# u's block built by ScalarE, fewer clearings, and another order of issue in an attention and two-MLP kernel

## The chip, the cores and the metric

The kernel runs on one core of a Trainium2 chip. The metric is the device time of one execution in microseconds (us). The profiler records one execution; its span runs from the first to the last instruction and is a little shorter than the execution's own time. The engines are named as in the profile: PE is TensorE's matmuls and PEld its weight loads, DVE is VectorE, ACT is ScalarE, POOL is GpSimd, SP is SyncE, on whose queue nearly all loads and stores are issued.

## The reference

All is fp32. A linear attention with a decay per channel runs over 768 steps, for 2 batches and 8 heads of 48 channels; its output, as 1536 tokens of 384 channels, goes through an MLP with ELU (2048 wide) and then through four experts (1024 wide, ReLU), whose outputs are weighted by normalized probabilities.

```python
    for t in range(S):
        kt, vt, rt, wt = (k[:, :, t], v[:, :, t], r[:, :, t], w[:, :, t])
        cur = np.einsum('bhd,bhe->bhde', u[None] * kt, vt)
        y[:, :, t] = np.einsum('bhd,bhde->bhe', rt, state + cur)
        state = wt[:, :, :, None] * state + np.einsum('bhd,bhe->bhde', kt, vt)
...
    h = x @ w_in
    g = np.where(h > 0.0, h, alpha * (np.exp(np.minimum(h, 0.0)) - 1.0))
    return (g @ w_out).astype(np.float32)
...
    p = domain_probs / (domain_probs.sum(-1, keepdims=True) + 1e-09)
    for e in range(E):
        h = np.maximum(x @ w1[e], 0.0)
        out += p[:, e:e + 1] * (h @ w2[e])
```

## The kernel before

**Attention.** The 768 steps are cut into chunks of 128: six for each batch, twelve in all, numbered 0 to 11 so that even ones belong to batch 0 and odd ones to batch 1 (`SEQ`). The eight heads lie in four pairs along the partitions (`heads`). A chunk `i` goes through small steps, each a function of `attn(i)` with a two-letter name that the order uses: `iw`, `ik`, `lv` load decays, keys with r, and v; `su` and `pr` are VectorE scans for the decays to the chunk's end and from its start; `kd` and `rd` multiply keys and r by them; `g` multiplies r by the keys in place; `tr` transposes kd on TensorE, with a ScalarE copy; `pa` are the scores; `ow` multiplies g by u's block, which sums it over a head's channels; `am` masks the scores, with VectorE (D), with a ScalarE copy and a GpSimd select (S), or one of each (M); `vo` multiplies ow's result by v; `pp` and `us` update the state, `ws` decays it; `py` multiplies masked scores by v and r by the state; `ys` adds vo's; `xs` splits the result into a rounded part (a ScalarE copy) and a rest (a subtraction); `xd` spreads rows of it by two DMAs.

**ELU block.** Tokens lie in three blocks of four chunks (`BLOCKS`). Step `n` of 48 stands for a quarter of the hidden width `q = n // 12`, the token block `n // 4 % 3`, and a tile `f = n % 4`. `h` is the first product (nine matmuls of 128x512, three passes of split operands for each of three parts of 128 channels) with ScalarE's ReLU and exponential, `e` the ELU on VectorE with a ScalarE copy of its rounded part, `el` the subtraction for its rest, `z` the second product (nine matmuls into three banks). `dr`, behind a quarter's fourth `z`, adds the banks to `x2`; in the last quarter it also splits the sum again into `x`, which the experts read: dr39 for block 0, dr43 for block 1, dr47 for block 2. The weights come as 32 pieces: `wl` loads one, `wa`, `wb` and `wc` take its words apart and split them.

**Experts.** For each expert and each token block eight first products (L468) alternate with second products (L442), one tile late; `hl` is a tile with the ReLU's rounded part (ScalarE, L471) and its rest (VectorE, L472). `load_w` splits the experts' weights with ScalarE copies and VectorE subtractions; four weight buffers (`wpool`) serve both blocks in turn, so an expert's weights can only be split once a buffer of the ELU block is free. The experts' code is not part of the order written by hand.

**What sets the order.** `ORDER` is a list of 565 steps, each a name, a number and, where there is a choice, the engine (A ScalarE, D VectorE, P GpSimd). `do` issues them in this order; every engine takes its own instructions in the order in which they were issued, and semaphores enforce the data dependences. The order before ends with `z47 dr47A dr39D`. The tile `a` of `pr` has one buffer, `kr` and `w` of the loads have two; PSUM has eight banks.

Ahead of the list stand the constants (L77 to L102): VectorE fills the scans' start values, GpSimd builds the masks, u2 (a column of u for each head of a pair) from u_sb, and `ublock` from u2 by broadcast copies. L168 to L171 clear four state tiles of 128x208, of which the last 16 columns are only ever read as padding.

Of the kernel before, what the change touches and what calls it, by code (L numbers as in the profile page):

```python
# [40 lines left out]
ik6 ys2 rd3D iw5 ow4 xs2P su6 us1 ow3 vo4 xs1P pa3 ik5 xd1 iw7 pr6 vo3 am3S kd6P rd6P py4 ws3A lv6 tr6A su5 tr3A wl2  # L41
wb0P g6P pp4 lv5 wb1D us4 py3 kd5P iw8 pp3 pr5 ys4 us3 ow6 tr5A pp6 ys3 pp5 rd5P pa5 ws6A wl17 xs3P wc1D ik7 wa2D xd3
g5P am5S wc0P wa3D su7 vo6 ik8 pr7 su8 pa6 xd2 iw9 am6M xs4P ow5 rd7P ws5A vo5 wb2D py5 kd7D wc2P wb3D py6 us5 us6 ws7A
kd8P tr7A g7P wc3P pa7 h2 wl19 wl18 ys6 ws8A h1 ys5 xd4 g8P lv7 xs5P ik9 ow7 su9 tr8A am7D wa17D wa18D pr8 e1 wb17D
rd8P pr9 el1P xs6P ow8 h0 vo7 wc17P lv8 e0 el0P py7 h3 pp8 pa8 kd9D pp7 iw10 xd5 rd9P us7 us8 tr9A ys7 z0 pa9 g9P xd6
iw11 z1 xs7P am8M lv9 e2 vo8 ik10 ws9D wa19D am9M su10 wb18P wb19P xd7 kd10P el2P ow9 vo9 pp9 g10P ik11 us9 py8 py9 wl4
# [18 lines left out]
def kernel_body(ctx, tc, wkr, vv, uu, w_in, w_out, w1, w2, dp, out):  # L65
# [125 lines left out]
    def attn(i):  # L191
# [62 lines left out]

        def own_scores():

            b["po"] = bank()
            for p in range(NPAIR):
                if i in SUMMED:
                    nc.tensor.matmul(b["po"][:, 2 * p:2 * p + 2], lhsT=b["k"][:, p], rhs=u2[:, p], start=True, stop=True)  # L260
                else:
                    nc.tensor.matmul(heads(b["po"])[:, p], lhsT=ublock[:, p], rhs=b["k"][:, p], start=True, stop=True)  # L262
# [11 lines left out]

        def own_values():

            if i in SUMMED:
                vo = tile_of("vo", 1, (P, 8, D))
                nc.vector.tensor_tensor(vo, b["vs"][:, 0:8 * D].rearrange("q (h d) -> q h d", h=8),
                                        b["po"][:, 0:8].unsqueeze(2).to_broadcast([P, 8, D]), ALU.mult)  # L280
            else:
                mul("D", tile_of("bv", 2), heads(b["po"]), b["v"])
# [18 lines left out]
        def values():  # L301
            b["py"] = py = heads_bank()

            both = [(p, j) for p in range(NPAIR) for j in range(2)]
# [4 lines left out]
            for p, j in both:
                h = 2 * p + j  # L310
                nc.tensor.matmul(py[64 * j:64 * j + 64, p, :], lhsT=b["vs"][:, D * h:D * h + 64],  # L311
                                 rhs=b[f"am{j}"][:, p, :], start=first and p == 0, stop=i not in SUMMED, skip_group_check=True)
            if i in SUMMED:
                for p, j in both:
                    nc.tensor.matmul(py[64 * j:64 * j + D, p, :], lhsT=b["vo"][:, 2 * p + j], rhs=ident,
                                     start=False, stop=True, skip_group_check=True)
# [288 lines left out]
```

## Time and profile before

| | us |
|---|---|
| median of 3 executions (706.32 to 708.93) | 706.48 |
| the profiled execution's own time | 706.21 |
| its span | 704.4 |
| PE busy | 669.3 |
| DVE busy | 338.5 |
| ACT busy | 235.8 |
| POOL busy | 194.3 |

A row of the page or of a table gives busy time and a count of instructions. In a timeline a row is a run of like instructions on one engine: its start, how long it lasted, engine, line, operation, output and input, and in brackets how long the engine had been idle ahead of it and what released it. PEclk is the clock that TensorE was granted, as a share of 2.4 GHz; the low level is half of that.

### The profile page before, as it was taken

The page shows a single profiled execution, that of the slowest core. Times are in us where ns is not written, and L with a number is a line of the kernel's source. Part 1 is how long each engine was busy: PE and PEld are TensorE (multiplying, and loading weights), DVE is VectorE, ACT ScalarE, POOL GpSimd, SP SyncE. Part 2 cuts the span into 40 slices and gives each one's busy share as a digit, 9 for nine tenths or more (in the row PEclk, how much of TensorE's full clock was granted, in tenths as well). Part 3 has the DMA queues.
Part 4 walks back from the last instruction along what each step waited for, and adds up shares of the span by engine and source line. Part 5 has one row for each costly group of instructions (what it writes and reads, how often), then busy time and mean ns, then how long its engine had stood idle before and what let it go on. Part 6 is the DMA issues. An engine that isn't in the chain of part 4 may idle for free.

```text
span 704.4 us, 8788 instructions
## 1 busy us (share of the span) xinstructions
PE 669.3 (95%) x3440; PEld 550.3 (78%) x3440; DVE 338.5 (48%) x518; ACT 235.8 (33%) x454; POOL 194.3 (28%) x166
## 2 busy tenths in 40 slices
PE   6877999999999999799999999999999999999994
PEld 4766878878888788678888888888888888888883
DVE  6876987756557763631223522123872134421212
ACT  1343554766556655511113311113311123211110
POOL 7696884124444343420000002020202020210200
PEclk8779999999999999989999999999999999999997
DMA  6645462552211220110001210002350001000101
GB/s 240 202 148 197 140 204 80 171 225 80 77 50 51 80 67 1 45 46 1 0 1 45 92 44 0 1 0 91 93 177 1 0 30 62 0 15 31 45 2 49
DMA packets 19383, 50.81 MB, mean 72 GB/s; under 512 B 2504, under 2 KB 3704, under 8 KB 19204
## 3 DMA queue, kind: packets, MB, share of 16 engines
q1 hardware_dynamic: 19188, 50.15, 22.4%
q8 instruction: 29, 0.48, 0.3%
q14 instruction: 22, 0.18, 0.1%
q10 hardware_dynamic: 144, 0.00, 0.0%
HBM read 46.58 MB, written 2.38 MB: 70 GB/s over the span
## 4 chain that ended last, share of the span: by engine, by line
PE 85%; POOL 5%; DVE 4%; DMA 2%; ACT 1%; issue 1%; POOLq 0%; DVEq 0%; ACTq 0%
PE bank L468 28%; PE bank L442 28%; PE bank L363 13%; PE bank L343 11%; POOL x L113 2%; PE bank L262 1%; PE bank L311 1%; PE bank L252 1%; PE bank L307 1%; DMA v<-in_vv 1%; POOL hl L113 1%; PE bank L245 1%; POOL am L272 1%; DMA raw<-in_w_out 1%; POOL kr L110 0%
## 5 line engine op out<-in xcount | busy, mean ns | idle before, releaser
L472 DVE SCALAR_TENSOR_TENSOR hl<-bank,hl 128x512 fp32r<-128x512 f32 x96 | 66.3, 690 | 257.9 <-ACT hl L471 254.1
L471 ACT ACTIVATE hl<-bank 128x512 fp32r<-128x512 f32 x96 | 57.4, 598 | 305.2 <-PE bank L468 305.2
L454 POOL TENSOR_TENSOR x<-o,x 128x512 f32<-128x512 f32 x24 | 31.1, 1320 | 333.0 <-DVE o L452 333.0
L343 PE MATMUL bank<-x,w 128*128 128x512 f32 x432 | 103.9, 391 | 1.3 <-DVE e L351 1.3
L363 PE MATMUL bank<-hl,w 128*128 128x512 f32 x432 | 104.2, 391 | 0.7 <-DVE e L351 0.3
L343 PEld LDWEIGHTS bank<-x,w 128*128 128x128 f32 x432 | 80.6, 188 | 18.8 <-ACT w L117 1.7
L363 PEld LDWEIGHTS bank<-hl,w 128*128 128x128 f32 x432 | 80.6, 188 | 18.7 <-ACT kdt L117 0.8
L468 PE MATMUL bank<-x,w_e0a 128*128 128x512 f32 x216 | 55.0, 400 | 5.0 <-POOL x L113 2.9
L351 DVE SCALAR_TENSOR_TENSOR e<-e,bank 128x512 f32<-128x512 f32 x48 | 32.4, 683 | 49.0 <-ACT e L347 48.9
L113 POOL TENSOR_TENSOR hl<-e,hl 128x512 fp32r<-128x512 f32 x28 | 39.9, 1428 | 49.8 <-ACT hl L117 43.4
L468 PEld LDWEIGHTS bank<-x,w_e0a 128*128 128x128 f32 x216 | 41.7, 194 | 14.7 <-POOL x L113 3.3
L468 PE MATMUL bank<-x,w_e2a 128*128 128x512 f32 x216 | 53.0, 390 | 0.0
L442 PE MATMUL bank<-hl,w_e0b 128*128 128x512 f32 x216 | 53.0, 389 | 0.0
L468 PE MATMUL bank<-x,w_e1a 128*128 128x512 f32 x216 | 52.9, 389 | 0.0
L442 PE MATMUL bank<-hl,w_e1b 128*128 128x512 f32 x216 | 52.9, 389 | 0.0
L442 PE MATMUL bank<-hl,w_e2b 128*128 128x512 f32 x216 | 52.9, 389 | 0.0
L468 PE MATMUL bank<-x,w_e3a 128*128 128x512 f32 x216 | 52.8, 389 | 0.0
L442 PE MATMUL bank<-hl,w_e3b 128*128 128x512 f32 x216 | 52.7, 389 | 0.0
L442 PEld LDWEIGHTS bank<-hl,w_e0b 128*128 128x128 f32 x216 | 40.5, 188 | 8.6 <-DVE hl L472 0.2
L468 PEld LDWEIGHTS bank<-x,w_e1a 128*128 128x128 f32 x216 | 40.5, 188 | 8.4
L442 PEld LDWEIGHTS bank<-hl,w_e3b 128*128 128x128 f32 x216 | 40.5, 188 | 8.4
L442 PEld LDWEIGHTS bank<-hl,w_e2b 128*128 128x128 f32 x216 | 40.5, 188 | 8.4
(101 smaller groups left out, 838.2 us busy)
## 6 DMA issues: line engine op xcount, KB each, us to landing
kr<-in_wkr SPq DMA_DIRECT2D x12, 512.0 KB, 3.9
raw<-in_w_in SPq DMA_DIRECT2D x16, 384.0 KB, 3.2
raw<-in_w_out SPq DMA_DIRECT2D x16, 384.0 KB, 3.4
v<-in_vv SPq DMA_DIRECT2D x12, 456.0 KB, 3.8
w<-in_wkr SPq DMA_DIRECT2D x12, 258.5 KB, 3.6
gw<-in_wkr SPq DMA_DIRECT2D x12, 258.0 KB, 2.7
pr<-rows SPq DMA_DIRECT2D x1, 3072.0 KB
out<-x SPq DMA_DIRECT2D x9, 256.0 KB, 2.0
```

The costliest lines, as they stand in the source:

```text
L113: engines[e].tensor_tensor(o, a, b.bitcast(F32), ALU.subtract)
L245: nc.tensor.transpose(pt[:, p, :], b["kd"][:, p, :], ident)
L252: nc.tensor.matmul(pa[j][:, p, :], lhsT=b["kd"][64 * j:64 * j + D, p, :], rhs=b["rd"][64 * j:64 * j + D, p, :], start=True, stop=True)
L262: nc.tensor.matmul(heads(b["po"])[:, p], lhsT=ublock[:, p], rhs=b["k"][:, p], start=True, stop=True)
L343: nc.tensor.matmul(ph, lhsT=wi[:, sa, f, kk, :], rhs=x[:, kk, c0:c0 + nch, sm], start=(kk == 0 and i == 0), stop=(kk == 2 and i == 2))
L351: nc.vector.scalar_tensor_tensor(b["e"], b["e"], -1.0, b["ph"], ALU.add, ALU.max)
L363: nc.tensor.matmul(pxs[q, bl][d], lhsT=wo[:, sa, f, d * P:(d + 1) * P], rhs=b["t"][:, sm], start=(f == 0 and i == 0), stop=(f == 3 and i = ...
L442: nc.tensor.matmul(sums[d], lhsT=w[:, sa, f % 4, d * P:(d + 1) * P], rhs=t[:, sm], start=(f == 0 and i == 0), stop=(f == 7 and i == 2))
L454: (nc.vector if last else nc.gpsimd).tensor_tensor(x2[:, d, s], o, x2[:, d, s], ALU.add)
L468: nc.tensor.matmul(ph, lhsT=wt_[:, sa, kk, (f % 4) * P:(f % 4 + 1) * P], rhs=x[:, kk, 4 * b:4 * b + 4, sm], start=(kk == 0 and i == 0), st ...
L471: nc.scalar.activation(out=t[:, 0, :], in_=ph, func=AF.Relu)
L472: nc.vector.scalar_tensor_tensor(t[:, 1, :], ph, 0.0, t[:, 0, :].bitcast(F32), ALU.max, ALU.subtract)
```

## The change

The constant `half` has ones in its two diagonal quarters of 64x64, and four ScalarE activations multiply it by u's columns to give `ublock`; u2 and its GpSimd copies go. One tile `sball` takes the place of the four state tiles, and one memset clears the last 16 columns of each; the rest of a state tile is written before it is read. A variant that no chunk used (`SUMMED` was empty) is deleted. The order is written anew: the same 565 steps, some on other engines, with the last quarter's dr39 between z39 and z47 instead of at the end.

```diff
 ORDER = """
-iw0 ik0 su0 kd0P pr0 rd0P g0P iw1 su1 pr1 pa0 lv2 ik1 wl0 lv0 wl16 ow0 rd1D kd1P am0M vo0 iw2 wa16D iw4 g1P ik2 wb16P
-ik4 su2 pa1 kd2P g2P tr0A wl1 lv1 iw3 pr2 tr1A py0 ow1 tr2A pp0 rd2P su4 ow2 am1M ys0 kd4P us0 pp2 xs0P ws2A ik3 pr4
-us2 pa2 vo1 pp1 am2M vo2 su3 rd4P g4D wa0D iw6 py1 wa1D wc16P kd3D py2 g3P pa4 xd0 wl3 am4S tr4A pr3 lv4 ys1 lv3 ws4A
...
-e43 e37 z36 h38 h44 e38 el43P z43 h39 el37D z37 el38P dr43D e39 el39P z38 e44 h47 el44P h46 z39 z44 e47 el47D z45 e46
-el46D z46 z47 dr47A dr39D
+iw0 su0 ik0 iw1 ik1 wl0 kd0P iw2 pr0 rd0P g0P su1 wl1 ow0 pr1 rd1P tr0A su2 pr2 wa0D wl16 wa16D lv0 ik2 lv2 kd1P iw4
+g1D pa0 rd2P pp0 am0D vo0 kd2P tr1A pa1 wb0P iw3 su4 ow1 g2P wl2 ik4 pr4 tr2A pa2 py0 am2S ow2 lv1 ys0 kd4P ik3 us0
+ws2A vo2 g4P wb16D su3 am1D pr3 rd4P iw5 xs0P pp2 py2 lv4 us2 pp1 ow4 ys2 kd3P ik5 tr4A rd3P wc0P vo1 py1 g3P ys1 us1
...
+e40 dr35D wc14P wb15D h37 z31 wa31D el40P e37 e41 wb31P wc15P el37P dr31D z40 h42 h38 e38 wc30D el41P e42 h43 z36 e43
+z37 h44 wc31P el42P el43P el38D z41 h39 e44 e39 z42 h46 z38 z43 el44D dr43D el39D h45 z44 e45 z39 el45P dr39A e46 h47
+z45 el46D z46 e47 el47D z47 dr47A
 """.split()
...
-    u2 = const.tile([P, NPAIR, 2], F32, name="u2")
-    nc.gpsimd.memset(u2, 0.0)
+    half = const.tile([P, P], F32, name="half")
+    nc.gpsimd.memset(half, 0.0)
     for j in range(2):
-        nc.gpsimd.tensor_copy(u2[64 * j:64 * j + 64, :, j:j + 1], u_sb[64 * j:64 * j + 64])
+        nc.gpsimd.memset(half[64 * j:64 * j + 64, 64 * j:64 * j + 64], 1.0)
     ublock = const.tile([P, NPAIR, P], F32, name="ublock")
     for p in range(NPAIR):
-        nc.gpsimd.tensor_copy(ublock[:, p].rearrange("q (j c) -> q j c", j=2), u2[:, p].unsqueeze(2).to_broadcast([P, 2, 64]))
+        nc.scalar.activation(out=ublock[:, p], in_=half, func=AF.Copy, scale=u_sb[:, p])
...
-    sb = [[apool.tile([P, 208], F32, name=f"sb{b}{i}") for i in range(2)] for b in range(2)]
-    for b in range(2):
-        for i in range(2):
-            nc.gpsimd.memset(sb[b][i], 0.0)
+    sball = apool.tile([P, 4, 208], F32, name="sball")
+    nc.gpsimd.memset(sball[:, :, NPAIR * D:], 0.0)
+    sb = [[sball[:, 2 * b + m] for m in range(2)] for b in range(2)]
```

## Rows read from the trace of the kernel before

**Rows 1.** The page: busy time, share of the span, instructions of TensorE.

```profile
PE 669.3 (95%) x3440; PEld 550.3 (78%) x3440; DVE 338.5 (48%) x518; ACT 235.8 (33%) x454; POOL 194.3 (28%) x166
```

**Rows 2.** Stages: length, busy us (instructions) by engine, granted clock, DMA share, GB/s.

```profile
0.00:90.00 90.00, 71.54 (x673) 57.75 (x673) 71.72 (x96) 34.62 (x80) 72.01 (x70) 0.85 0.58 189
90.00:288.00 198.00, 196.39 (x1009) 161.85 (x1010) 125.42 (x200) 117.63 (x220) 82.56 (x67) 1.00 0.30 93
288.00:306.31 18.31, 13.27 (x49) 10.01 (x47) 11.72 (x15) 6.22 (x12) 8.70 (x6) 0.81 0.29 86
306.31:693.03 386.72, 386.72 (x1708) 319.91 (x1707) 125.73 (x203) 77.34 (x143) 31.05 (x24) 1.00 0.11 33
```

**Rows 3.** Timeline from 284 to 307 us, where the experts begin.

```profile
284.38 10.36 PE L363 MATMUL bank<-hl,w 128*128 128x512 f32 x45
...
293.42 3.85 DVE L372 TENSOR_TENSOR x<-bank,x 128x512 f32<-128x512 f32 x6 [3.11 <-PE bank L363]
...
294.86 8.70 POOL L113 TENSOR_TENSOR x<-x,x 128x512 fp32r<-128x512 f32 x6 [10.23 <-ACT x L117]
...
296.92 0.73 PE L468 MATMUL bank<-x,w_e0a 128*128 128x512 f32 x2 [2.17 <-ACT x L117]
297.18 5.24 DVE L113 TENSOR_TENSOR w_e0b<-raw_e0b,w_e0b 128x384 fp32r<-128x384 f32 x4
...
300.51 5.80 PE L468 MATMUL bank<-x,w_e0a 128*128 128x512 f32 x16 [2.86 <-POOL x L113]
```

**Rows 4.** Timeline of the first 14 us: SyncE, VectorE, GpSimd and ScalarE.

```profile
1.26 0.42 SPq L210 DMA_DIRECT2D kr<-in_wkr  x1
...
3.86 1.23 DVE L223 TENSOR_TENSOR_SCAN z<-w,first 128x516 f32<-128x516 f32 x1 [1.29 <-DMA w<-in_wkr]
...
4.07 1.25 POOL L99 COPY u<-u_sb 64x4 f32<-64x4 f32 x2 [2.05 <-DMA u_sb<-in_uu]
...
5.69 2.62 POOL L102 COPY ublock<-u 128x128 f32<-128x128 f32 x4
6.49 1.25 DVE L223 TENSOR_TENSOR_SCAN z<-w,first 128x516 f32<-128x516 f32 x1
...
8.26 0.47 POOL L171 MEMSET sb<- 128x208 f32 x2
8.70 1.17 POOL L110 TENSOR_TENSOR kd<-kr,z 128x512 f32<-128x512 f32 x1
...
11.04 2.28 DVE L230 TENSOR_TENSOR_SCAN a<-w,start 128x516 f32<-128x516 f32 x1 [3.08 <-POOL rd L110]
...
12.20 2.11 POOL L110 TENSOR_TENSOR kd<-kr,z 128x512 f32<-128x512 f32 x1
...
13.21 0.60 ACT L117 ACTIVATE am<-bank 128x512 f32<-128x512 f32 x1 [10.69 <-PE bank L252]
```

**Rows 5.** Timeline at 245 us: a short wait of TensorE inside the ELU block.

```profile
245.52 2.30 PE L343 MATMUL bank<-x,w 128*128 128x512 f32 x9 [1.26 <-DVE e L351]
```

**Rows 6.** Groups up to 300 us: busy us, mean ns | idle before; DMA: size, landing.

```profile
L125 ACT ACTIVATE sb<-sb,z 128x48 f32<-128x48 f32 x36 | 9.0, 327 | 0.0
...
L110 DVE TENSOR_TENSOR am<-bank,mask 128x512 f32<-128x512 f32 x12 | 7.9, 676 | 2.0 <-PE bank L252 2.0
...
kr<-in_wkr SPq DMA_DIRECT2D x12, 512.0 KB, 3.9
```

**Rows 7.** Waits of TensorE and SyncE: us in total, times, longest us.

```profile
PE bank L245 <- POOL kd L110: 4.7, 1, 4.7
...
PE bank L292 <- DMA v<-in_vv: 3.4, 2, 2.4
...
SPq L210 <- PE bank L262: 17.7, 7, 6.6
```

**Rows 8.** Timeline at 29 us: the decayed r of chunk 4 on GpSimd.

```profile
29.28 1.18 POOL L110 TENSOR_TENSOR rd<-kr,a 128x512 f32<-128x512 f32 x1
```

**Rows 9.** Timeline at 71 us: the first two first products of the ELU block.

```profile
71.50 4.39 PE L343 MATMUL bank<-x,w 128*128 128x512 f32 x18
```

More of the change, by code (lines that the diff above doesn't have):

```diff
@@ L32 @@
 WARM = 3
-SUMMED = set()
 ORDER = """
-iw0 ik0 su0 kd0P pr0 rd0P g0P iw1 su1 pr1 pa0 lv2 ik1 wl0 lv0 wl16 ow0 rd1D kd1P am0M vo0 iw2 wa16D iw4 g1P ik2 wb16P
-ik4 su2 pa1 kd2P g2P tr0A wl1 lv1 iw3 pr2 tr1A py0 ow1 tr2A pp0 rd2P su4 ow2 am1M ys0 kd4P us0 pp2 xs0P ws2A ik3 pr4
-us2 pa2 vo1 pp1 am2M vo2 su3 rd4P g4D wa0D iw6 py1 wa1D wc16P kd3D py2 g3P pa4 xd0 wl3 am4S tr4A pr3 lv4 ys1 lv3 ws4A
-ik6 ys2 rd3D iw5 ow4 xs2P su6 us1 ow3 vo4 xs1P pa3 ik5 xd1 iw7 pr6 vo3 am3S kd6P rd6P py4 ws3A lv6 tr6A su5 tr3A wl2
@@ L42 @@
[L42 to L46, printed above, removed]
@@ new lines @@
+g1D pa0 rd2P pp0 am0D vo0 kd2P tr1A pa1 wb0P iw3 su4 ow1 g2P wl2 ik4 pr4 tr2A pa2 py0 am2S ow2 lv1 ys0 kd4P ik3 us0
+ws2A vo2 g4P wb16D su3 am1D pr3 rd4P iw5 xs0P pp2 py2 lv4 us2 pp1 ow4 ys2 kd3P ik5 tr4A rd3P wc0P vo1 py1 g3P ys1 us1
+xd0 pa4 xs2P ws4A iw6 am4D su5 wl3 pa3 xs1P ik6 tr3A lv3 vo4 am3S xd1 xd2 su6 iw7 pp4 lv5 kd5P ow3 pr6 ws3A wa1D wa3D
+vo3 us4 wb1P py4 rd6P kd6D wb3P pp3 lv6 ik7 g5P ws6A py3 pr5 ys4 ys3 wc1D us3 g6P su7 xs3P pa6 xd3 wc16D rd5P tr5A tr6A
+am6M ow6 vo6 ws5A xs4P wa2D ow5 pp5 iw8 pa5 kd7D py6 ik8 lv7 ys6 pp6 g7P am5S tr7A ow7 us5 us6 pr7 vo5 wl18 su8 lv8
@@ new lines @@
+rd7P kd8D wb2P wc2P xs6P py5 ys5 h0 ws8A pr8 wl19 iw9 ik9 wl17 pa7 ws7A wc3D wa18D xd4 h1 wl4 wa19D am7D vo7 e1 wb18P
+rd8P tr8A pp7 lv9 g8P us7 e0 h3 el1P su9 xd6 py7 wa17D xs5P h2 el0D pa8 ow8 kd9D z0 ik10 wb17P am8D e2 iw10 wc17P g9D
+vo8 pp8 iw11 py8 pr9 ws9A us8 e3 tr9A ys7 ys8 el2D rd9P xs7D su11 wb19P wc19D xd5 z1 el3D xd7 wc18P pa9 ik11 ow9 wl6
+vo9 am9S xs8P su10 pp9 lv11 kd10P pr10 z2 g10P us9 kd11P rd10D g11P wl20 py9 z3 dr3A h4 pr11 e4 lv10 wl5 h5 ys9 pa10
+ws11A h6 rd11P el4D ws10A ow11 xs9P wa4D pa11 wa6D vo11 am11D am10D ow10 e5 wb4P el5P vo10 z4 wb6D wc6P xd8 h7 py10
@@ new lines @@
+ys10 xd9 xs10P py11 wc4D wl21 e7 z5 e6 wl7 el7D ys11 xs11D h14 xd10 wa20D wa5D el6P h12 wa7D wb20P wb7P z6 e12 xd11 |
+wl23 z7 wa21D e14 wb5D h8 wc7P el14P dr7D el12D wc5D e8 wl22 wl8 h9 h11 wa22D e9 el8P wl11 el9P wb22D h10 wl10 z8 e10
+el10D wl24 wc20P h13 wb21D e11 wa23D e13 wc21P h17 el13D z9 h16 z10 z12 el11P wb23D wa11D e16 el16P e17 z11 z13 wa8D
+wc22P wl9 wc23D wl25 dr11A h20 h15 wl26 z14 wb11D z16 e20 el17P wa10D wl27 e15 wb8P wc11P el15D h21 wa24D wc8P wb10P
+z15 h18 el20D e21 z17 dr15A wa9D wb9D h22 wc10P wa25D e18 wb24D el21P e22 wc24P z20 h19 e19 h23 el18P z18 e23 el19D
@@ new lines @@
+el22P z21 wa26D h28 wc9P wb26D wl12 wa27D h24 e28 z22 el23D z19 h27 wb27P dr19D e24 wc26D h25 z23 wa12D el24D dr23D z24
+wb25P el28P wl14 wl28 e25 e27 h29 wb12D el25P h26 e29 wc27P wc25D e26 wl13 h32 el27P wl29 e32 wl30 el26D el32D wc12D
+z28 z25 h34 wa13D el29P e34 z29 z26 h33 h35 z27 e33 el34P wa28D dr27A h30 z32 wa29D wb13D e35 el33P wb28P z33 wa14D e30
+h31 el35D wb14P wl15 wb29P wc13P wc28D e31 wl31 el30D h36 el31P wc29P z34 wa30D wa15D e36 h40 el36P z30 z35 h41 wb30P
+e40 dr35D wc14P wb15D h37 z31 wa31D el40P e37 e41 wb31P wc15P el37P dr31D z40 h42 h38 e38 wc30D el41P e42 h43 z36 e43
@@ L255, in own_scores @@
         def own_scores():
-            b["po"] = bank()
+            b["po"] = heads_bank()
             for p in range(NPAIR):
[L259 to L262, printed above, removed]
+                nc.tensor.matmul(b["po"][:, p], lhsT=ublock[:, p], rhs=b["k"][:, p], start=True, stop=True)
         def masked(e):
@@ L275, in own_values @@
         def own_values():
[L277 to L282, printed above, removed]
+            mul("D", tile_of("bv", 2), b["po"], b["v"])
         def decayed_s(e):
@@ L311, in values @@
                 nc.tensor.matmul(py[64 * j:64 * j + 64, p, :], lhsT=b["vs"][:, D * h:D * h + 64],
[L312 to L316, printed above, removed]
+                                 rhs=b[f"am{j}"][:, p, :], start=first and p == 0, stop=True, skip_group_check=True)
         def results():
@@ L321, in parts @@
         def parts(e):
-            split(i, b["py"] if i in SUMMED else b["bv"], e)
+            split(i, b["bv"], e)
         return {"iw": load_decays, "ik": load_kr, "lv": load_v, "su": suffixes, "pr": prefixes, "kd": decayed_k, "rd": decayed_r, "g": own,
```

15 lines of the change are left out of this document (1 added, 14 removed).

## The prediction

> **What bounds the kernel now.** I read the page's busy shares first: TensorE is busy for 669.3 of 704.4 us, 95% [rows 1]. So only time in which TensorE stands still or runs at its low clock can be won, and the stages tell where that is [rows 2]. From 306.31 to 693.03 us it is busy in every microsecond at granted clock 1.00; from 90 to 288 us it is idle for 1.61 of 198 us. Two stages are left. In 0 to 90 us, the attention, it is idle for 18.46 us at a mean granted clock of 0.85, while VectorE and GpSimd are busy for 71.7 and 72.0 us each: they, and the order in which they work, set the pace. In 288 to 306.31 us, where the experts begin, it is idle for 5.04 us at 0.81. The timeline of that place shows why [rows 3]: the last second product of the ELU block ends at 284.38 + 10.36 = 294.74 us, and only then come the sums of token blocks 2 and 0 (dr47, dr39: six VectorE adds, with six ScalarE copies and six GpSimd subtractions behind them). The experts' first products read block 0, whose sums stand last. TensorE waits 2.17 us, runs two matmuls, waits 2.86 us for GpSimd, then runs sixteen in 5.80 us. The start is the third view [rows 4]: GpSimd builds u's block and clears tiles until 8.73 us, and its first decayed key starts at 8.70 us although the scan that it needs ended at 3.86 + 1.23 = 5.09 us.
>
> **The change, part by part.**
>
> *The end of the ELU block.* dr39A moves from behind dr47A to between z39 and z47. Behind z39 TensorE still has h47, z45, z46 and z47, four groups of 9 matmuls. Nine take about 2.04 us (45 in 10.36 us [rows 3] is 2.07 for nine), so 8.2 us. dr39 needs three adds, of which the first takes 3.85/6 = 0.64 us, one ScalarE copy (0.60 us for 128x512 [rows 4]), and three subtractions at 8.70/6 = 1.45 us [rows 3]: 0.64 + 0.60 + 3 x 1.45 = 5.6 us. Block 0 is ready with 2.6 us to spare, and the work that hides it is those four groups; without that cover the three subtractions alone would cost 4.4 us. On each queue something now stands behind dr39: e46 on VectorE (two more us until it starts), e46's copy and h47's exponential on ScalarE, only dr47 on GpSimd. z46 wants e46 4.1 us behind z39; adds, ELU, copy and rest are 1.9 + 0.7 + 0.6 + 0.7 = 3.9 us: just in time, and half a microsecond of it is in the 1.5 us below. What is won at most: from 294.74 us to the end of the sixteen at 300.51 + 5.80 = 306.31 us lie 11.57 us for 18 matmuls that take 4.08 us elsewhere, so 7.49 us.
>
> What is late next: the first lower half `hl` on VectorE. w_e0b's second half goes into the buffer that z47 frees, so four ScalarE copies and four VectorE subtractions stand at this same place; beside GpSimd's x work those four took 5.24 us on VectorE [rows 3]. In the new order TensorE is done with two groups of first products at 4.08 us behind z47 and wants `hl` then. VectorE has two adds of dr47 left there and three of GpSimd's subtractions beside it. If the four subtractions go ahead of `hl` at 1.31 us, `hl` is done at about 1.3 + 5.2 + 0.7 = 7.2 us, a stall of 3.1; if they go behind it, none. I take 1.5 us, the middle, for the trace doesn't show which comes first. A stall of 1.26 us at 245.5 us left the nine matmuls behind it at 2.30 us [rows 5], so I add nothing for the clock. **The end gives 7.5 - 1.5 = 6.0 us (3 to 7.5).**
>
> *The start.* From GpSimd go: two small copies of u (1.25 us) with the wait for u_sb ahead of them (2.05), four copies of 128x128 (2.62) and five clearings, two of which took 0.47 us [rows 4]. Added: three memsets of at most 128x128 and one of 4x16 columns; at 0.24 us each, as those clearings of 128x208, under 1 us, and before anything waits for them. ScalarE gets four activations of 128x128 with a scale from a tile. The nearest rows are 128x48 with such a scale (327 ns [rows 6]) and a copy of 128x512 (0.60 us [rows 4]), so 1.3 to 2.4 us, from about 4 us on (the copies that read u_sb began at 4.07 us, as it landed [rows 4]). That ends by 6.5 us; ScalarE is idle until 13.21 us [rows 4], and the reader, own_scores, comes after the first g at 9 us or later. It costs nothing; without that cover it would cost its 2.4 us.
>
> So kd0 can begin when its scan (5.09) and its keys are there: issued at 1.26 us, with a median of 3.9 us to landing [rows 4, 6], 5.2 us. That is 3.5 us earlier than 8.70. But pr0's scan then runs beside it. In the trace a scan beside GpSimd's copies took 1.25 us, a scan beside a product of two tiles 2.28, and that product's successor 2.11 us where 1.17 is the short one [rows 4]: the two take turns. So 2.28 - 1.23 = 1.05 us comes off. **The start gives 3.5 - 1.0 = 2.5 us.**
>
> The Trainium skill (GPSIMD Engine Reference, section 1, Specifications) says that GpSimd's SBUF interfaces are shared with VectorE, with contention where VectorE has two SBUF inputs; by that rule what goes (copies of one input) had been nearly free and what moves up is not. The trace agrees in the 2.28 against 1.25 us. How far this goes is the first rival below.
>
> *The order of the head.* I counted both lists. Products of two tiles and subtractions on GpSimd: rd 8 to 11, wb 16 to 19, wc 19 to 20, g 11 to 10, xs 11 to 10, el 28 to 26, so 3 more; its masks go from 12 to 9 selects. At 1.17 us or more for a product, and less for a select, that is 1 to 2 us more over 290 us, and VectorE loses about as much. With the short times (scan 1.23 us, product 1.17 on GpSimd [rows 4], 0.68 on VectorE [rows 6]) the VectorE and GpSimd work ahead of the first hidden product is 88.8 us in the old list and 91.4 in the new one, ahead of z1 112.6 and 122.9, ahead of h4 132.9 and 136.3. The two engines together got through (71.7 + 72.0)/90 = 1.6 busy us per us [rows 2], so the new list is 1.6, 6.4 and 2.1 us behind the old one at these three points, if neither waits less or more than before. That is its one disadvantage in the counts; between z0 and z1 TensorE has other chunks' products to run, and it is at h4 again near the old one. Against it stand the two longest waits that a better order could take away, 4.7 us for kd4 and 2.4 us for v [rows 7]. I set the order at 0, between a loss of 6.4 us and a gain of 7.1: it is nearer to neither end.
>
> One wait is added: pr3 now stands on VectorE ahead of rd4P in the list, and `a` has one buffer, so VectorE waits at pr3 until GpSimd has done kd4P, g4P and rd4P. Behind it on VectorE stand us2, ys2, vo1, ys1 and am4. Before, rd4 ran from 29.28 to 30.46 us, with kd4 and the subtraction of xs0 ahead of it [rows 8]. With one product (g4, 1.2 us) put ahead of it and the start 2.5 us earlier it ends near 29 us; VectorE has 20.2 us of short work ahead of pr3, from 3.86 us on, and with its waits is there at 28 to 30 us. I take 0 to 1 us, inside the zero above.
>
> On SyncE, iw2 stands ahead of lv0 and waits for pr0. v0's issue so moves to about 9 us and lands near 13 (3.9 us, the median of the loads of that size [rows 6]). It is first wanted by pp0, behind own_scores, transposes and scores of chunk 0 on TensorE, which cannot begin before g0 near 10 us: nothing, and if those three were done sooner, pp0 and vo0 would wait for it, 1 us perhaps.
>
> **Sum.** The profiled execution takes 706.21 us for a span of 704.4; the median is 706.48, 0.3 above. 706.2 - 6.0 - 2.5 + 0 = 697.7, plus 0.3: **698.0 us**. About 0.5% (3.5 us) is what a measurement of this kernel can tell from no change.
>
> **The rivals.**
> 1. *The port takes the start.* If all three scans of the start meet a product on GpSimd, 3 x 1.05 = 3.2 of the 3.5 us go: 706.5 - 6.0 - 0.3 = 700.2 us. For it: the 2.28 us. Against: VectorE also loses a wait of 3.08 us at 11.04 us [rows 4].
> 2. *The order also fills the head.* If it takes away most of the two waits of 7.1 us, some 5.5 us more: 692.5 us. Against: the list's own counts above.
> 3. *The gap at the experts changes its owner.* The w_e0b subtractions stand ahead of `hl` for 3.1 us, and the clock falls as in the trace, where 16 matmuls took 5.80 instead of 3.6 us: 2.2 more. Then the end gives 2.2 us: 706.5 - 2.2 - 2.5 = 701.8 us. The Trainium skill (TensorE: Matmul & The Clock Gate, Part 1) says that the throttled state is the default and activity releases it; the trace agrees with 0.81 behind the gap and no fall behind the 1.26 us.
> 4. *Slower: the knot at pr3.* rd4P waits for chunk 4's keys, whose buffer own_scores of chunk 1 frees; SyncE waited up to 6.6 us for that product [rows 7]. Each microsecond that rd4P ends later than VectorE's arrival at pr3 is lost to all of VectorE's queue. It eats the whole gain at 8.5 us (rd4P ending at about 38 us) and makes the kernel slower by over 0.5% from 12 us, rd4P at about 42 us: 710 us or more. At 5 to 11 us it ends within 0.5% of before, as would the 6.4 us that z1 may be late. Against: it ended at 30.46 us before.
>
> **How the numbers follow.** Chances: forecast 0.41 (its own range 695.5 to 699.5), port 0.18, fuller head 0.18, gap with a new owner 0.08, knot or late z1 at no measurable change 0.10, slower 0.05. Faster by over 0.5% is 0.41 + 0.18 + 0.18 + 0.08 = 0.85. The range goes from the low end of the fuller head, 690.5, to 703.0 and leaves 0.15 and a little out.
>
> **What would show it.** In the new trace: kd0 on GpSimd at about 5.2 us, pr0's scan stretched beyond 2 us; the ELU block's last second product followed by the experts' first with under 0.3 us between, then at most one wait of `hl` of 0 to 3 us with granted clock 1.00; TensorE idle in the first 90 us some 2.5 us less. It is wrong if pr3 waits for more than 2 us, if the first hidden product begins less than 2 us ahead of the old one's 71.50 us [rows 9], or if TensorE's waits between 90 and 288 us exceed 3 us.

## The result, and the profile after

The changed kernel takes 695.45 us (median of 4 executions, 694.18 to 696.66) against 706.40 for the kernel before in the same comparison (4 executions, 704.84 to 708.93): a ratio of 0.9841 with a 95% interval of 0.9819 to 0.9863. Two later comparisons, among the experiments below, gave 0.9861 and 0.9855. So 10 to 11 us are gone, where 8.5 were forecast; 695.45 lies between the forecast of 698.0 and the rival "the order also fills the head" (692.5), each about as far off, and just outside the forecast's own range (695.5 to 699.5). The profiled execution took 696.66 us for a span of 694.9, so the two traces compared here differ by 9.5 us.

The page of the kernel after, the line that answers to [rows 1]:

```profile
PE 669.0 (96%) x3440; PEld 549.5 (79%) x3440; DVE 346.7 (50%) x517; ACT 238.0 (34%) x459; POOL 192.2 (28%) x159
```

TensorE's busy time is the same to 0.3 us. Its waits have gone, not its work. The stages of the kernel after, columns as in [rows 2]; the third stage ends with the first nine second products of the experts, where that of [rows 2] ends with the first products ahead of them, and the fourth is what follows:

```profile
0.00:90.00 90.00, 76.85 (x714) 62.32 (x715) 79.48 (x103) 37.09 (x88) 66.95 (x62) 0.83 0.61 197
90.00:288.00 198.00, 197.72 (x991) 161.63 (x989) 129.99 (x197) 119.61 (x221) 89.78 (x71) 1.00 0.28 90
288.00:298.88 10.88, 8.54 (x36) 6.57 (x36) 8.44 (x11) 4.52 (x9) 4.43 (x3) 1.00 0.49 146
298.88:683.50 384.62, 384.62 (x1699) 318.21 (x1698) 124.95 (x202) 76.73 (x142) 31.04 (x24) 1.00 0.11 34
```

In the first 90 us TensorE is idle for 13.15 us instead of 18.46, from 90 to 288 us for 0.28 instead of 1.61, and in the third stage the granted clock is 1.00 where it was 0.81. The 5.31 us less of idle time at the start, where 2.5 were forecast, are not all a gain: the clock there is 0.83 instead of 0.85, and part of what looks busy is the same work done at the low level.

The start in the timeline of the kernel after (start, duration, engine, line, operation, output and input, idle time ahead and its releaser), beside [rows 4]:

```profile
3.95 1.28 ACT L101 ACT_TABLE_LOAD   x1 [3.95 <-DMA u_sb<-in_uu]
...
5.13 1.18 POOL L109 TENSOR_TENSOR kd<-kr,z 128x512 f32<-128x512 f32 x1 [3.13 <-DVE z L219]
5.29 2.11 DVE L226 TENSOR_TENSOR_SCAN a<-w,start 128x516 f32<-128x516 f32 x1
...
6.25 0.34 POOL L98 MEMSET half<- 64x64 f32 x2
6.63 1.28 ACT L101 ACTIVATE ublock<-half,u_sb 128x128 f32<-128x128 f32 x4 [1.39 <-POOL half L98]
7.32 1.20 DVE L219 TENSOR_TENSOR_SCAN z<-w,first 128x516 f32<-128x516 f32 x1
...
7.54 1.95 POOL L109 TENSOR_TENSOR rd<-kr,a 128x512 f32<-128x512 f32 x1 [0.95 <-DVE a L226]
...
9.53 2.28 DVE L226 TENSOR_TENSOR_SCAN a<-w,start 128x516 f32<-128x516 f32 x1 [0.79 <-POOL rd L109]
...
10.77 2.08 PE L255 MATMUL bank<-kr,ublock 128*128 128x128 f32 x8 [3.54 <-POOL kr L109]
```

kd0 begins at 5.13 us instead of 8.70, and pr0's scan beside it takes 2.11 us instead of 1.23: both as forecast. u's block takes ScalarE 1.28 us and ends before GpSimd's product of r is done.

The boundary of the ELU block and the experts, the same kind of timeline, beside [rows 3]:

```profile
281.48 4.26 POOL L112 TENSOR_TENSOR x<-x,x 128x512 fp32r<-128x512 f32 x3
...
283.12 4.86 PE L347 MATMUL bank<-hl,w 128*128 128x512 f32 x19
...
284.51 1.65 DVE L112 TENSOR_TENSOR w_e0b<-raw_e0b,w_e0b 128x384 fp32r<-128x384 f32 x1
...
286.68 1.48 DVE L112 TENSOR_TENSOR w_e0b<-raw_e0b,w_e0b 128x384 fp32r<-128x384 f32 x3
...
287.81 0.40 PE L452 MATMUL bank<-x,w_e0a 128*128 128x512 f32 x1
...
288.81 2.14 PE L347 MATMUL bank<-hl,w 128*128 128x512 f32 x8 [0.61 <-DVE hl L112]
...
290.79 4.03 PE L452 MATMUL bank<-x,w_e0a 128*128 128x512 f32 x17
...
293.00 3.34 DVE L112 TENSOR_TENSOR w_e0b<-raw_e0b,w_e0b 128x384 fp32r<-128x384 f32 x3 [0.26 <-ACT w_e0b L116]
...
296.27 1.28 DVE L456 SCALAR_TENSOR_TENSOR hl<-bank,hl 128x512 fp32r<-128x512 f32 x2
297.00 1.88 PE L426 MATMUL bank<-hl,w_e0b 128*128 128x512 f32 x7 [1.73 <-DVE hl L456]
```

Block 0's three subtractions (L112 on GpSimd) end at 285.74 us, 5 us before the ELU block's last second product. That one ends at 288.81 + 2.14 = 290.95 us, and the experts' first products follow without a gap. What is left is one wait of 1.73 us for the experts' `hl`, which stands on VectorE behind w_e0b's subtractions (the row at 293.00), and a new one of 0.61 us inside z47.

TensorE's waits over the kernel after, the two longest (total, times, longest), beside [rows 7]:

```profile
PE bank L255 <- POOL kr L109: 4.7, 3, 3.5
PE bank L280 <- DMA v<-in_vv: 3.2, 1, 3.2
```

The wait of 4.7 us for a decayed key and both waits for `x` are gone. v's longest wait grew from 2.4 to 3.2 us. The key was not kd4's, as the prediction has it: in the kernel before, the wait stands ahead of the transposes of chunks 6 and 3, for the fifth decayed key that GpSimd makes there, kd6 (at 44.95 us; kd4 ran at 26.32).

```profile
47.09 1.97 PE L245 MATMUL bank<-ident,kd 128*128 128x128 f32 x8 [4.74 <-POOL kd L110]
```

**How the traces are compared below.** Three points divide a trace well: the start of the first hidden product, the end of the ELU block's last second product, and the end of the first nine second products of the experts. Each is the start of a timeline row, or a start plus a duration. The end of the block and of the nine products are the same work in all kernels. The first hidden product, and with it the column of the ELU block, is comparable only between kernels with the same order: the new one puts attention work between the first two hidden products.

| kernel (its profiled execution) | first hidden product | end of ELU block | nine second products done | ELU block | boundary |
|---|---|---|---|---|---|
| before | 71.50 | 294.74 | 308.46 | 223.24 | 13.72 |
| before, dr39 moved (e1) | 70.01 | 297.86 | 305.58 | 227.85 | 7.72 |
| before, dr39 moved, w_e0b's rests on GpSimd (e8) | 71.22 | 297.60 | 303.55 | 226.38 | 5.95 |
| before, new constants (e2) | 69.07 | 290.81 | 304.85 | 221.74 | 14.04 |
| new order, old constants, dr39 last (e11) | 69.31 | 291.39 | 305.25 | 222.08 | 13.86 |
| new order, new constants, dr39 last (e3) | 67.04 | 289.06 | 302.62 | 222.02 | 13.56 |
| new order, old constants (e4) | 69.51 | 293.01 | 300.95 | 223.50 | 7.94 |
| the same (e12) | 68.33 | 291.53 | 299.46 | 223.20 | 7.93 |
| after | 67.79 | 290.95 | 298.88 | 223.16 | 7.93 |
| the same (e9) | 67.34 | 290.82 | 298.77 | 223.48 | 7.95 |
| the same (e13) | 68.09 | 291.55 | 299.50 | 223.46 | 7.95 |
| after, w_e0b's rests on GpSimd (e5) | 66.06 | 288.91 | 295.11 | 222.85 | 6.20 |
| the same (e10) | 67.18 | 289.93 | 296.15 | 222.75 | 6.22 |
| after, more warming matmuls (e6) | 66.30 | 289.59 | 297.54 | 223.29 | 7.95 |

The last two columns hardly scatter between executions of one kernel (0.02 us in the boundary of after, 0.3 us in its ELU block). The scatter that these traces show lies in the first 70 us: kernels that are the same up to the first hidden product reach it 1.5 us apart (before, e1, e8), 1.2 us apart (e11, e4, e12) and 2.0 us apart (after, e9, e13, e3, e5, e10).

### The profile page after: what moved, and what is told of

It is laid out like the page before. It is cut to its first block, busy times and chain, and to the rows that moved or that the text cites. A ratio compares the mean times of both kernels' runs of the same rounds, so it can differ in the third digit from the quotient of the medians.

```text
span 694.9 us, 8786 instructions
## 1 busy us (share of the span) xinstructions
PE 669.0 (96%) x3440; PEld 549.5 (79%) x3440; DVE 346.7 (50%) x517; ACT 238.0 (34%) x459; POOL 192.2 (28%) x159
## 4 chain that ended last, share of the span: by engine, by line
PE 91%; DVE 3%; POOL 2%; issue 1%; DMA 1%; ACT 1%; SPq 0%; DVEq 0%; POOLq 0%
PE bank L426 28%; PE bank L452 28%; PE bank L327 14%; PE bank L347 13%; PE bank L255 2%; PE bank L248 2%; PE bank L299 1%; PE bank L295 1%; POOL kr L109 1%; PE bank L280 1%; PE bank L241 1%; DVE w_e0b L112 1%; DVE a L226 0%; POOL rd L109 0%; DMA v<-in_vv 0%
## 5 line engine op out<-in xcount | busy, mean ns | idle before, releaser
L327 PEld LDWEIGHTS bank<-x,w 128*128 128x128 f32 x432 | 80.5, 188 | 18.2 <-DVE e L335 1.1
L452 PE MATMUL bank<-x,w_e0a 128*128 128x512 f32 x216 | 52.9, 389 | 0.0
L112 POOL TENSOR_TENSOR hl<-e,hl 128x512 fp32r<-128x512 f32 x26 | 35.9, 1383 | 55.2 <-ACT hl L116 54.6
L452 PEld LDWEIGHTS bank<-x,w_e3a 128*128 128x128 f32 x216 | 40.6, 188 | 8.4
```

Of the source, the lines that this page charges most:

```text
L112: engines[e].tensor_tensor(o, a, b.bitcast(F32), ALU.subtract)
L327: nc.tensor.matmul(ph, lhsT=wi[:, sa, f, kk, :], rhs=x[:, kk, c0:c0 + nch, sm], start=(kk == 0 and i == 0), stop=(kk == 2 and i == 2))
L452: nc.tensor.matmul(ph, lhsT=wt_[:, sa, kk, (f % 4) * P:(f % 4 + 1) * P], rhs=x[:, kk, 4 * b:4 * b + 4, sm], start=(kk == 0 and i == 0), st ...
```

## Experiments

The first theory is the prediction's: dr39's place gives 6.0 us, the constants 2.5, the order of the rest nothing. Against it stand its rivals, above all that the order also fills the head. Kernels compared with each other ran on the same chip where the text gives a difference of ratios, unless it says otherwise.

**dr39 alone, in the old list (e1).**

```diff
-... h46 z39 z44 e47 el47D z45 e46
-el46D z46 z47 dr47A dr39D
+... h46 z39 dr39A z44 e47 el47D z45 e46
+el46D z46 z47 dr47A
```

> The kernel before with one step moved: dr39A from the end to behind z39. The prediction's theory (the wait of 7.5 us at the experts' start is block 0's late sums, and 1.5 us of it comes back as a wait for hl): 6.0 us less than before (3 to 7.5), so about 700.4 us, and no wait of TensorE for x left at the experts' start. Rival (the gain of the changed kernel comes mostly from the rearranged head): under 2 us less.

Measured: 705.23 us (10 executions), ratio 0.9991 (0.9969 to 1.0012). That is a miss of 5.4 us, and of 3.8 at the least. Its timeline at the boundary:

```profile
287.11 3.92 DVE L113 TENSOR_TENSOR w_e0b<-raw_e0b,w_e0b 128x384 fp32r<-128x384 f32 x3
...
289.48 1.52 PE L468 MATMUL bank<-x,w_e0a 128*128 128x512 f32 x6
...
293.00 0.50 PE L363 MATMUL bank<-hl,w 128*128 128x512 f32 x1 [2.00 <-ACT hl L117]
...
301.24 0.96 PE L442 MATMUL bank<-hl,w_e0b 128*128 128x512 f32 x3 [1.11 <-ACT hl L471]
...
303.92 1.66 PE L442 MATMUL bank<-hl,w_e0b 128*128 128x512 f32 x6 [1.49 <-DVE hl L472]
```

The gap for `x` is gone and the boundary is 6.00 us shorter (7.72 for 13.72), but the ELU block is 4.61 us longer. dr39's subtractions on GpSimd now meet w_e0b's on VectorE, which take 3.92 us for three at 287.11; e46 stands behind them, ScalarE's copy waits 3.82 us for it, and TensorE 2.00 us for the copy in the middle of the last second products. Some of the 6.00 us is no gain either: eight of the experts' first products (six at 289.48 and two later ones) were run inside the ELU block. Most of what is saved behind the block is lost within it: 6.00 - 4.61 leaves 1.4 us by the traces.

**The same with w_e0b's rests on GpSimd (e8).** If those subtractions on VectorE are the new owner, moving them away should bring the step's price back.

```diff
-                    sub("D", w[:, 1, s], raw[:, DM * q:DM * q + DM], w[:, 0, s])
+                    sub("P" if nm[:3] == "e0b" else "D", w[:, 1, s], raw[:, DM * q:DM * q + DM], w[:, 0, s])
```

> The order before with dr39A behind z39, as in the run of that step alone, and w_e0b's eight subtractions on GpSimd. Theory (moved alone, dr39 gained little because its VectorE adds and GpSimd subtractions there made w_e0b's subtractions, and with them the rest of steps 46 and 47 and hl, late): waits of 2.0, 1.5 and 1.1 us at the end go, about 3 to 4 us less than that run, 3 to 5 less than before. Rival (the old tail is slow by itself): no more than 1 us less than that run.

Measured: 700.64 us (8 executions), ratio 0.9923 (0.9898 to 0.9948), 4.8 us below e1 by the ratios (on another chip). The rows of the same place:

```profile
292.12 0.50 PE L363 MATMUL bank<-hl,w 128*128 128x512 f32 x1 [1.05 <-ACT hl L117]
...
300.98 0.96 PE L442 MATMUL bank<-hl,w_e0b 128*128 128x512 f32 x3 [0.21 <-ACT hl L471]
```

The waits of 2.00, 1.11 and 1.49 us became 1.05, 0.21 and nothing, with one of 0.36 us new inside the block; by the table block and boundary are 3.2 us shorter together. This confirms that in e1 the gap had passed to w_e0b's subtractions on VectorE.

**The constants alone, in the old list (e2).** The edit is the hunks of the diff on `half`, `ublock` and `sball`, with the old `ORDER`.

> The kernel before with the constants alone changed: u's block by ScalarE from half, one memset of 4x16 columns instead of four clearings; the old order stays. The prediction's theory: the first decayed key starts 3.5 us earlier, 1 us of it is lost to the scan beside it: 2.5 us less than before, about 704 us. Rival (GpSimd's products beside VectorE's scans take it back): 0.3 us less. Second rival (TensorE at its low clock holds the head, not VectorE and GpSimd): under 1 us less though the first key starts 3.5 us earlier.

Measured: 703.66 us (10 executions), ratio 0.9952 (0.993 to 0.9975): 3.4 us (1.8 to 4.9), with the forecast 2.5 inside the interval.

**The changed kernel with dr39 at the end (e3).**

```diff
-... z39 el45P dr39A e46 h47
-z45 el46D z46 e47 el47D z47 dr47A
+... z39 el45P e46 h47
+z45 el46D z46 e47 el47D z47 dr47A dr39A
```

> The changed kernel with dr39A put back to the end, behind dr47A. The prediction's theory: 6 us more than the changed kernel (3 to 7.5), near 701.5 us, with TensorE waiting for x about 5 us in two pieces and a granted clock near 0.8 behind it. Rival (in the new order the sums of block 0 aren't what the experts wait for): under 2 us more.

Measured: 701.81 us (8 executions), ratio 0.9947 (0.9927 to 0.9967). Against the three comparisons of the changed kernel (0.9841, 0.9861, 0.9855, on another chip or in another call) that is 6 to 7.5 us slower. The old gap is back in its timeline:

```profile
291.23 0.79 PE L452 MATMUL bank<-x,w_e0a 128*128 128x512 f32 x2 [2.17 <-ACT x L116]
...
294.79 5.69 PE L452 MATMUL bank<-x,w_e0a 128*128 128x512 f32 x16 [2.77 <-POOL x L112]
```

From the end of the ELU block at 289.06 us to the end of the eighteen first products at 300.48 are 11.42 us; in the kernel after they end at 294.82, 3.87 us behind the block. So the gap that the move takes away is worth 7.55 us, as the prediction worked out (7.49), and 1.73 of it come back as the wait for `hl`. But the move also makes the ELU block longer, by 1.1 to 1.5 us in every pair of the table with the new order. e3's rows at the block's end show where:

```profile
282.31 4.47 PE L347 MATMUL bank<-hl,w 128*128 128x512 f32 x19
...
283.61 0.56 DVE L112 TENSOR_TENSOR w_e0b<-raw_e0b,w_e0b 128x384 fp32r<-128x384 f32 x1 [2.35 <-ACT w_e0b L116]
...
284.20 0.69 DVE L335 SCALAR_TENSOR_TENSOR e<-e,bank 128x512 f32<-128x512 f32 x1
...
286.95 2.11 PE L347 MATMUL bank<-hl,w 128*128 128x512 f32 x8 [0.17 <-DVE hl L112]
```

In the kernel after, w_e0b's first subtraction there takes 1.65 us (the row at 284.51) beside block 0's on GpSimd, where here it takes 0.56. e47 stands behind it on VectorE and begins 2.96 us after the start of the nineteen second products (286.08 - 283.12), here 1.89. So the nineteen take 4.86 us instead of 4.47, and the last eight wait 0.61 us instead of 0.17. Net the move brings 13.7 - 7.9 - 1.3 = 4.5 us by the traces.

**The changed kernel with the old constants (e4, and again e12).** The edit puts back the four GpSimd copies, u2 and the four clearings.

> The changed kernel with the constants of before: GpSimd builds u2 and u's block and clears four tiles; the new order stays. The prediction's theory: the first decayed key starts at about 8.7 us again, 2.5 us more than the changed kernel, near 698 us. Rival (own_scores stand first on TensorE in the new order, and wait for g0 alone): the same or up to 3.5 us more. Second rival (the low clock holds the head): under 1 us more.

> The changed kernel with before's constants, beside the changed kernel itself on the same chip. If the constants are worth 2 to 3.5 us in any order, this one is 0.003 to 0.005 above it in the ratio; if the new order hides most of what u's block costs on GpSimd, it is 0 to 0.002 above it.

Measured: 697.60 us (4 executions), ratio 0.9871 (0.9842 to 0.99); again 697.82 us (6 executions), ratio 0.989 (0.9868 to 0.9913), beside the changed kernel at 0.9855 on the same chip. In the new order the constants are worth 0.0035, some 2.5 us with an uncertainty of about as much.

**The order alone (e11), and the changed kernel beside it (e13).** e11 has the old constants and dr39 behind dr47: neither of the two steps that the prediction gave a value.

```diff
 (new ORDER, and in it)
-... z39 el45P dr39A e46 h47
-z45 el46D z46 e47 el47D z47 dr47A
+... z39 el45P e46 h47
+z45 el46D z46 e47 el47D z47 dr47A dr39A
 (u2, ublock and the four clearings as before)
```

> The new order with neither of its two companions: before's constants on GpSimd, and dr39A behind dr47A at the end. What is left against the kernel before is the order of the head and of the ELU block alone. By the prediction this is worth 0: ratio 1.000 (0.997 to 1.003). By the theory formed from the runs so far, which leave about 1.6 to 2.5 us over when the constants' part and dr39's part are taken out, the ratio is 0.9965 to 0.998, and the first hidden product stays ahead of 71.5 us by 1 us or more, with the two waits for the experts' x (2.2 and 2.8 us) back in the trace.

> The changed kernel unaltered, as the companion of the two others: ratio 0.984 to 0.987. Less the order alone, the difference is what dr39's move and the constants bring together in the new order: about 0.011 to 0.013 by the theory from the runs, 0.012 by the prediction (8.5 us).

Measured: e11 701.10 us (6 executions), ratio 0.9928 (0.9909 to 0.9946), so 5.1 us (3.8 to 6.4) from a part that the prediction had set at 0 and the later theory at about 2. e13 gave 696.08 us (5 executions), ratio 0.9855. Between the two lie 0.0073, 5.2 us, for dr39's place and the constants together, where 8.5 were expected. The stretches of the head in e11, columns as in the stages above:

```profile
30.00:67.00 37.00, 28.50 (x370) 24.64 (x369) 34.50 (x46) 15.88 (x41) 31.35 (x24) 0.93 0.66 192
67.00:90.00 23.00, 23.00 (x225) 18.27 (x225) 22.59 (x32) 13.54 (x32) 16.59 (x14) 1.00 0.62 197
```

The stretches of the kernel before that answer to these, not among the rows ahead of the prediction:

```profile
30.00:67.00 37.00, 30.16 (x351) 26.04 (x349) 27.99 (x40) 14.54 (x37) 27.80 (x22) 0.80 0.58 182
67.00:90.00 23.00, 19.77 (x175) 15.71 (x170) 22.23 (x30) 13.03 (x29) 19.62 (x15) 1.00 0.50 156
```

From 30 to 67 us VectorE and GpSimd did 27.99 + 27.80 = 55.8 busy us in the old order and 34.50 + 31.35 = 65.9 in the new one, 1.51 and 1.78 per us: of the 74 us of the two engines 18.2 and 8.2 were idle. TensorE has 3.2 us less idle time from 67 to 90 us, and from 30 to 67 us more clock (0.93 for 0.80). GpSimd's two longest waits between 30 and 67 us in the kernel before:

```profile
POOL x L113 <- ACT x L117: 4.9, 1, 4.9
POOL kr L110 <- DVE kd L110: 4.3, 1, 4.3
```

and in e11:

```profile
POOL kr L109 <- PE bank L281: 1.6, 1, 1.6
POOL x L112 <- ACT x L116: 1.6, 1, 1.6
```

The 4.3 us were GpSimd's product g3 waiting for kd3, which the old list gives to VectorE and the new one to GpSimd itself. But this stretch is the one in which the new order does best. In the first 30 us it is the other way round, 46.1 busy us of the two engines in the kernel before (first row) and 41.0 in e11 (second row):

```profile
0.00:30.00 30.00, 21.60 (x157) 16.00 (x159) 21.50 (x27) 7.05 (x14) 24.59 (x35) 0.80 0.64 221
0.00:30.00 30.00, 19.27 (x117) 13.91 (x118) 21.12 (x26) 5.58 (x9) 19.89 (x32) 0.81 0.59 198
```

The first hidden products of the table measure the whole head. With the old constants they begin at 71.50, 70.01 and 71.22 us in the old order (before, e1, e8) and at 69.31, 69.51 and 68.33 in the new one (e11, e4, e12): 1.9 us earlier in the means. That the new order is ahead is so shown by the times and the traces; which of the waits it owes this to is not, for no run changes one of them alone.

The pair e11 and e12, on one chip, is also the second price of dr39's place: 0.0038 by the ratios, 2.7 us (3.3 in the medians), where e3 gave 6 to 7.5. The 4.5 us of the traces lie between the two, so the times leave the size of this part open between 2.7 and 7.5 us.

**w_e0b's rests on GpSimd in the changed kernel (e5, and again e10 beside e9, the changed kernel unaltered).** The edit is that of e8. It asks whether the 1.73 us of wait are what the prediction said they are.

> The changed kernel with the eight subtractions for w_e0b on GpSimd instead of VectorE. Theory (what is late at the experts' start is hl, and z47's rest ahead of it, behind w_e0b's subtractions on VectorE): the waits of 1.7 us (hl, L456) and 0.6 us (L112) go, about 2 us less than the changed kernel. Rival (GpSimd with dr47's subtractions and these is late for the products that need w_e0b): up to 3 us more, and TensorE waits for POOL w_e0b.

> The changed kernel itself, on the same chip as the next run, for a comparison of the two: a ratio of 0.984 to before, as at first (0.982 to 0.986). If the waits at the experts' start are the same in every execution: 1.7 us for hl and 0.6 us for the rest of step 47 again, whatever the granted clock of the head.

> The changed kernel with w_e0b's eight subtractions on GpSimd, a second time, beside the changed kernel on the same chip. Theory (its 2.0 us at the experts' start are real, and the medians of the first time were too far apart in chips to show them): a ratio 0.002 to 0.003 lower than the changed kernel's. Rival (the gain is given back later, or was the head's clock): the same ratio within 0.001.

Measured: e5 694.52 us (6 executions), ratio 0.9835 (0.9811 to 0.9859). e9 696.60 (6 executions), ratio 0.9861 (0.9839 to 0.9883), and e10 on the same chip 694.33 (6 executions), 0.9834 (0.9808 to 0.986): 2.3 us in the medians, though the intervals overlap. The timeline of e5:

```profile
286.77 2.14 PE L347 MATMUL bank<-hl,w 128*128 128x512 f32 x8 [0.71 <-DVE hl L112]
...
292.83 2.28 PE L426 MATMUL bank<-hl,w_e0b 128*128 128x512 f32 x9
```

and its rows on GpSimd and VectorE ahead of z47:

```profile
284.17 4.39 POOL L112 TENSOR_TENSOR w_e0b<-raw_e0b,w_e0b 128x384 fp32r<-128x384 f32 x4
...
285.17 1.54 DVE L112 TENSOR_TENSOR hl<-e,hl 128x512 fp32r<-128x512 f32 x1 [1.00 <-ACT hl L116]
```

No wait stands ahead of the experts' second products any more, and the boundary is 1.7 us shorter in both executions; the ELU block is 0.3 to 0.7 us shorter. z47's wait stayed, at 0.71 us, with another owner: the subtraction for its `hl` takes 1.54 us beside w_e0b's on GpSimd, where it took 0.68 in the kernel after. The nineteen products ahead of it take 4.47 us again. e9 and e13 repeat the waits of the kernel after, 1.74 and 0.61 us. This version is the fastest of all that ran.

**The clock in the head (e6).** In the kernel after the granted clock is 0.53 from 12 to 32 us. More warming matmuls on TensorE ahead of the attention would show whether that holds the head up.

```diff
-WARM = 3
+WARM = 8
```

> The changed kernel with 8 warm-up products on TensorE instead of 3, so that it stays busy until about 10.8 us, when own_scores begin. Theory of the low clock: from 12 to 32 us TensorE is busy for 18.6 of 20 us at half clock, so it holds the head there; with a granted clock of 1.00 in that stretch the head ends 2 to 4 us earlier, so 691 to 693 us. Rival, the prediction's (VectorE and GpSimd hold the head): under 1 us either way though the clock is higher. Third (the clock falls again in the first waits): granted clock 0.5 from 14 us on and no difference.

Measured: 696.49 us (6 executions), ratio 0.9865 (0.9835 to 0.9895), no difference from e9. The stretch from 12 to 32 us of e6:

```profile
12.00:32.00 20.00, 16.46 (x193) 14.41 (x191) 17.54 (x22) 6.53 (x14) 14.43 (x12) 0.83 0.62 199
```

and of the kernel after:

```profile
12.00:32.00 20.00, 18.57 (x146) 16.00 (x147) 15.45 (x18) 5.33 (x12) 13.34 (x11) 0.53 0.54 178
```

The clock rose from 0.53 to 0.83 and TensorE's busy time fell by 2.1 us although it did more matmuls there. The time did not fall measurably, where the theory wanted 2 to 4 us. So a TensorE that is busy for 93% of a stretch need not be what ends last in it. A gain of a microsecond is not excluded: the trace of e6 has its first hidden product at 66.30 us, early among the 66.06 to 68.09 of the six traces with the head unaltered. And a part of the gain may have been paid for: the longer warming let own_scores of chunk 0 begin at 11.98 us instead of 10.77.

## Why the prediction was right, and where it was not

**The sign, the range and the time held**; the sum was 1.3 to 2.5 us short. Two of its three terms were mis-sized, and the errors went opposite ways; that the sum came so near is in part luck.

**The gap at the experts** was read correctly: 7.55 us of it against 7.49, the wait for `hl` behind w_e0b's subtractions 1.73 us against 1.5, the granted clock 1.00. e5 and e10 show the cause of that wait by taking it away. The term's size was off at the other end. The prediction called z46's need of e46 "just in time" and counted the block's waits inside the 1.5 us. z46 came in time, but z47 did not: e47 stood behind w_e0b's first subtraction, which GpSimd's work for block 0 had stretched to 1.65 us, and the ELU block became 1.3 us longer. By the traces the term is 4.5 us net, not 6.0; by the times it is 2.7 or 6 to 7.5.

**Moving dr39 is worth its price only with what goes with it.** Alone in the old list it gave 0.6 us by the times (at most 2.2) and 1.4 by the traces; the prediction's sentence that each queue gets "something behind dr39" had the right list, and missed what happens when w_e0b's subtractions, which the list by hand doesn't contain, come into the middle of it: in e1 they stand ahead of e46.

**The start** came as worked out: kd0 at 5.13 us (5.2), the scan 2.11 us (beyond 2), the constants 3.4 us (1.8 to 4.9) in the old order and about 2.5 in the new one, against 2.5. A rival's mechanism is there too: pr1's scan at 9.53 us is also stretched, to 2.28 us. One argument was wrong without harm. The two memsets of `half`'s quarters were to run before anything waits for them; they ran behind kd0, at 6.25 us, and u's block waited for them.

**The order of the head** is the step that failed. The prediction counted the work on VectorE and GpSimd and divided it by the 1.6 busy us per us of the kernel before, "if neither waits less or more than before". By that the order had the first hidden product 1.6 us late; it came 1.9 us early in the means of three traces each. Alone the order gave 5.1 us (3.8 to 6.4) by the times, and in the profiled executions the ELU block ends 3.35 us earlier with it. Between 30 and 67 us the two engines waited less (8.2 us idle where it had been 18.2), in the first 30 us more (19.0 for 13.9). The rate itself is a weak measure: up to the first hidden product it is 1.53 in the trace of before (109.2 busy us in 71.50) and 1.64 in that of e1 (114.5 in 70.01), which is the same kernel up to there. In the kernel after the idle time of 1.61 us from 90 to 288 us, with the wait of 1.26 us [rows 5] in it, is down to 0.28 as well, which the prediction had not counted. The rival of the fuller head had the direction right. Of the two waits that it named one is gone, of kd6 and not of kd4, and the other, of v, is longer than before.

**The wait at pr3** was no added wait. With rd4P put ahead of pr3 in the list each engine gets the same instructions in the same order, since the two steps stand on different engines and pr3 needs `a` free either way. pr3's scan in the kernel after shows no idle time ahead of it:

```profile
34.55 1.22 DVE L226 TENSOR_TENSOR_SCAN a<-w,start 128x516 f32<-128x516 f32 x1
```

The fear of z1 did not come true either: from 67 to 90 us TensorE has no idle time in e11, in which the order is alone, where before it had 3.2 us.

**What stays open.** Alone the parts give 0.6 + 3.4 + 5.1 = 9.1 us, together 10 to 11, within their errors. But e3, which has the constants and the order, is not faster than e11, which has the order alone (0.9947 and 0.9928, on two chips), though its profiled execution reaches every point of the table 2.3 to 2.6 us earlier. By the times the order's share is 5.1 us (e11) or 0.4 (e3 against e2). The traces are closer to each other: up to the nine second products the order brings 3.2 us with the old constants (e11 against before) and 2.2 with the new ones (e3 against e2), each from one execution. In the table's first column the means even add up: the constants take 1.8 us off in either order, and the order 1.8 to 1.9 with either constants. So the order's sign and rough size are settled, its mechanism is not. Whether the constants and the order share a gain in some executions, or a chip or two unlucky sets of executions make this, no run tells.

## What to carry to other kernels

Before a step is moved out of a gap, write down all that will stand at its new place on each engine, including what an automatic scheduler puts there: the same move was worth nothing measurable in one list and, by the traces, some 4.5 us in another, and moving w_e0b's subtractions to another engine added 4.8 and 2.3 us. Busy time divided by the present rate prices a new order only if the waits stay, so list the waits of the engines that set the pace in that stretch, not only TensorE's, and ask which of them the new order removes. Undo each part in the new kernel and also do it alone in the old one, since the two answers can differ by the whole price.

## What the hardware showed

A product of two tiles on GpSimd and a scan on VectorE took turns in these rows, and the one that started second paid for both. pr0's scan began 0.16 us behind kd0 and took 2.11 us, kd0 its usual 1.18; at 7.32 us the scan began first and took 1.20 us, and the product of r behind it 1.95. The Trainium skill (GPSIMD Engine Reference, section 1, Specifications) states that the two engines share their SBUF interfaces; the rows here agree, and in them the second to start is the one that waits. The contention that it names goes by VectorE's inputs, and the scan has two beside copies and products alike; so that GpSimd's copies let the scan pass (1.25 us [rows 4]) stands on the row alone, and not on that rule, as the prediction has it. Subtractions of 128x384 on VectorE went from 0.49 us (1.48 for three at 286.68) to 1.11 and more beside GpSimd's subtractions (3.34 for three at 293.00).

ScalarE's table load, the first thing on that engine in the kernel before, stands behind the landing of u_sb in the kernel after, at 3.95 us, ahead of the first activation that reads it. In the kernel before it ran at 1.24 us. Here that cost nothing, since `half` came later still. The row of the kernel before:

```profile
1.24 1.28 ACT L117 ACT_TABLE_LOAD   x1 [1.24 <-PEq L593]
```

The granted clock of TensorE in the head was no measure of the head's cost: e6 raised it from 0.53 to 0.83 over 20 us, and the time did not change measurably (0.9865 against 0.9861).
